# Strassen's scheme for every token pair of the last down projection

## The chip, the core and the metric

The kernel runs on one core of a Trainium2 chip. The core has a matrix engine (TensorE, "PE" in the profile), a vector engine (VectorE, "DVE"), a scalar engine (ScalarE, "ACT"), GpSimd ("POOL") and SyncE ("SP"), which here issues the transfers. Each engine takes its instructions in their order and waits on semaphores that other engines or transfers raise. The metric is the device time of one execution in microseconds (us); the time of a kernel is the median over its runs.

## The reference

One transformer block over 2048 tokens of width 1024, all inputs in bfloat16:

```python
mod = (_silu(c) @ w_mod).reshape(c.shape[0], 6, 1, -1)      # sa, ca, ga, sb, cb, gb
h = _layernorm(x) * (1 + ca) + sa
x = x + ga * _A_ref(h, A_wqkv, A_wo)      # linear attention, 32 heads of 32
h = _layernorm(x) * (1 + cb) + sb
x = x + gb * _B_ref(h, B_w_gate, B_w_up, B_w_down)
# _B_ref: _gelu(x @ w_gate) * (x @ w_up) @ w_down
```

The feed-forward network (FFN) has an inner width of 3584: `w_gate` and `w_up` are 1024 x 3584, `w_down` is 3584 x 1024. The change concerns the last product, the multiplication by `w_down` (the down projection), for the second half of the tokens.

## The kernel before

All engines' work is recorded by a small scheduler class (`Sched`): every operation names the bytes that it reads and writes, and the semaphore waits follow from that. Within an engine the order of the recorded calls is the order of execution (one early stretch of the program is reordered by a planner; the part that matters here is not). On-chip memory is one arena with offsets given by hand (`OFF_...`), so many tiles share bytes over time: a tile can be written when the last reader of what lay there is done.

The 2048 tokens are 16 chunks of 128 (c0 to c15). After attention, the FFN runs in two halves `p` of 1024 tokens. A half first runs 14 units `u`, each for 256 of the 3584 inner columns, and then the down projection of its eight chunks, with `w_down` cut into 28 K tiles of 128 rows (`fc`), loaded as seven tiles `wd0` to `wd6` of four K tiles, 1 MB each (`wd_dma`).

**A unit** (`unit`, L1449 on) multiplies by Strassen's scheme in Winograd's form: operands are cut 2 x 2, seven products take the place of eight, and sums of blocks are formed before and after. TensorE runs the products in the order 1, 5, 6, 2, 7, 3, 4, each for gate and up (t = 0, 1) with four matmuls of 512 columns (L1426). Products 1 and 2 use blocks as they are, in bf16; the others use sums, kept in fp32r. VectorE makes the weight sums of the next unit (`t_sum`, L1401), the additions after products 6 and 7 (`padd`, L1437) and the products yT = gelu(gate) * up (L1446); ScalarE makes the gelu (L1442), copies of partial results (L1431, L1434) and the fp32r copy of one weight block (L1390). The result `yT` stays on chip as the stationary operand of the down projection.

**The loads of w_down in the second half.** `wd0` and `wd1` are still on chip from the first half. `wd2` lies on the buffer of the gate and up weights of the last unit but one and is loaded behind that unit. `wd5`, `wd3`, `wd6` and `wd4` are issued in this order at the end of the last unit. Each waits until the tile below it has been read: `wd5` until product 6, `wd3` until product 2, `wd6` until product 3, `wd4` until product 4.

**The down projection of the second half** (the `if p:` branch) works on pairs of chunks; a pair has four results of 128 x 512 (two chunks by two halves of the output), each in one PSUM bank, so two pairs fill the eight banks. The first pair (c8, c9) is direct: for `wd0`, `wd1`, `wd2`, `wd5`, `wd3`, `wd6`, `wd4` in turn, 16 matmuls each (`down`, L1511). Meanwhile VectorE forms the weight sums `dt` (`d_t`, L1540) of K tiles 0 to 11 and, for the next pair, the sums of `yT` (`d_s`, L1567). The other three pairs (`d_pair`) run those 12 K tiles by Strassen's scheme: the K tiles are taken in six pairs (`NDJ = 6`), rows and columns being the two chunks, the two K tiles of a pair and the two halves of the output; seven products (`d_prod`, L1581) of six matmuls each make 42 in place of 48. The other 16 K tiles are added directly, 64 matmuls. After product 1 ScalarE copies the result to a second bank (L1599), after product 5 it copies to the tile `de` (L1601), and VectorE adds after products 6 and 7 (`d_add`, L1589). A finished bank is multiplied by the gate, added to x (`evac`, L1503 and L1504), and stored (L1506). In the last pair the last bank is cut into pieces of 320, 128 and 64 columns (`TAIL`), so that little remains behind the last matmul.

The tiles of the sums: `dt` has 15 tiles of 2 x 512 fp32r, `ds0` and `ds1` hold the first two sums of `yT`, and the other three of `yT` lie in `dha` and `dhb`, the right halves of `wd0`, `wd1` and `wd2`, whose direct reading is over by then.

Of the kernel before, what the change touches and what calls it, by code (L numbers as in the profile page):

```python
# [319 lines left out]
def bass_adaLN_cond__linear_attn_block__geglu_ffn__prompt_kernel(  # L320
# [16 lines left out]
    with ExitStack() as es:  # L337
# [1170 lines left out]
        def down(c_, k, b, c0, c1, fcs, first, last):  # L1508
            ci, n, o = c_ % (2 * CPG), c1 - c0, None
            for fc in fcs:  # L1510
                o = sch.op(T, lambda e, fc=fc: e.matmul(PS(b, 0, n), YT[:, yrow(fc), ci * P:(ci + 1) * P], WDT[fc // 4][:, fc % 4, c0:c1],  # L1511
                                                        start=first and fc == fcs[0], stop=last and fc == fcs[-1], skip_group_check=True),
                           rd=r_yt(fc, ci * P, (ci + 1) * P) + r_wd(fc), pwr=(pr(b) if first and fc == fcs[0] else ()), note=f"down c{c_} k{k} fc{fc}")
# [13 lines left out]
        def r_dt(q, i):  # L1527
            return [(OFF_DT[q][i], OFF_DT[q][i] + 4096, f"dt{q}{i}")]

        def d_t(q, i):  # L1530
            w = WDT[q].ap().rearrange("p (j r) d -> p j r d", r=2)
            b = lambda r, cc: w[:, :, r, cc * 512:(cc + 1) * 512]
            rb_ = lambda r, cc: [(WDQ[q] + (2 * j + r) * 2048 + cc * 1024, WDQ[q] + (2 * j + r) * 2048 + (cc + 1) * 1024, f"wd{q}") for j in range(2)]
            t32 = lambda k: DT[q][k].ap().bitcast(f32)
# [5 lines left out]
            sch.op(V, lambda e: e.tensor_tensor(DT[q][i][:], in0, in1, ALU.subtract), rd=rd, wr=r_dt(q, i), note=f"dtsum {q}.{i}")  # L1540
# [244 lines left out]
```

## Time and profile before

| | |
|---|---|
| median of 3 runs | 798.46 us (798.2 to 798.8) |
| profiled execution | 798.54 us |
| its span, first to last instruction | 796.3 us |
| TensorE busy | 789.3 us (99%), 3987 matmuls |
| VectorE busy | 595.8 us (75%) |
| ScalarE busy | 312.2 us (39%) |
| FFN units of the second half | up to 699.2 us, 12.6 each |
| down projection of the second half | 699.2 to the end |

How the lines are read: "L1511 PE MATMUL ps_all<-wd,yT ..." names the line of the kernel, the engine, the operation, the tile written and the tiles read. A group's line gives the count, the busy time, the mean of one in ns, and the idle time of the engine ahead of it with what ended it. In the timeline a row is: start, duration, engine, line, operation, shape, count, and in brackets the idle time before it. The chain of work that ended last is followed back from the last instruction: at each step to what released it, or to the instruction ahead of it on its engine; in order of time a row is start, duration, engine and line. Matmuls are pipelined, so a matmul's duration (379 ns) is longer than the time from one start to the next; times of a stream are therefore taken from the chain or from starts.

### The profile page before, as it was taken

Reading aid. Unit: us, or ns where it says so; the run is one execution under the profiler, and the core shown is the slowest. Engines: PE = TensorE matmul, PEld = TensorE weight load, DVE = VectorE, ACT = ScalarE, POOL = GpSimd, SP = SyncE. Lnnn points to the kernel's source line nnn. Section 1 sums busy time; section 2 is a strip of 40 time slices with the busy share of each in tenths; the row PEclk is TensorE's granted clock in tenths of the full one; section 3 lists DMA queues with packets and bytes.
Section 4 is the critical chain, followed back from the end, with each engine's and each line's share of the span. In section 5 each row is a group of like instructions: output and inputs, shape, how many; then the busy total and the mean of one; then the engine's idle time right before and its main releaser. Section 6 shows DMA issues by size and latency. Waiting matters only on the chain.

```text
span 796.3 us, 10865 instructions
## 1 busy us (share of the span) xinstructions
PE 789.3 (99%) x3987; PEld 470.2 (59%) x3987; DVE 595.8 (75%) x1046; ACT 312.2 (39%) x526; POOL 40.4 (5%) x102
## 2 busy tenths in 40 slices
PE   8999999999999999999999999999999999999998
PEld 4444445666445776767775444467776777745555
DVE  6799898894889978878776374577878878885433
ACT  2497743333574434444353411033534444321000
POOL 2121200000420000000001000000000000000000
PEclk9999999999999999999999999999999999999999
DMA  9789849849996153323228234022332323340000
GB/s 287 242 177 234 172 110 243 196 89 203 221 266 183 54 152 112 106 55 104 83 77 244 47 80 106 20 87 74 86 103 56 107 55 104 106 158 28 27 27 26
DMA packets 161340, 97.72 MB, mean 123 GB/s; under 512 B 68476, under 2 KB 148612, under 8 KB 160264
## 3 DMA queue, kind: packets, MB, share of 16 engines
q1 hardware_dynamic: 161272, 97.04, 47.4%
q8 instruction: 31, 0.51, 0.3%
q14 instruction: 21, 0.17, 0.1%
q10 hardware_dynamic: 16, 0.00, 0.0%
HBM read 78.92 MB, written 4.47 MB: 105 GB/s over the span
## 4 chain that ended last, share of the span: by engine, by line
PE 94%; DVE 2%; SPq 2%; DMA 1%; issue 0%; DVEq 0%
PE ps_all L1426 44%; PE ps_all L1511 20%; PE ps_all L883 7%; PE ps_all L919 7%; PE ps_all L868 6%; PE ps_all L1252 5%; PE ps_all L1581 4%; SPq L585 1%; DMA wmq<-in_w_mod_dram 1%; DVE xall L1266 1%; SPq L590 1%; DVE tp L1401 0%; PE ps_all L901 0%; PE ps_all L1184 0%; DVE ss L1381 0%
## 5 line engine op out<-in xcount | busy, mean ns | idle before, releaser
L1426 PE MATMUL ps_all<-ss,tp 128*128 128x512 f32 x896 | 224.4, 402 | 0.4 <-DVE ss L1381 0.4
L1426 PEld LDWEIGHTS ps_all<-ss,tp 128*128 128x128 f32 x896 | 168.3, 188 | 41.0 <-DVE ss L1381 1.1
L1511 PE MATMUL ps_all<-wd,yT 128*128 128x512 bf16 (+3 forms) x784 | 163.3, 370 | 0.0
L1511 PEld LDWEIGHTS ps_all<-wd,yT 128*128 128x128 bf16 x784 | 74.7, 98 | 87.8 <-issue 0.8
L1442 ACT ACTIVATE ge<-ps_all 128x512 f32<-128x512 f32 x112 | 64.1, 597 | 142.8 <-DVE ps_all L1437 81.0
L1426 PE MATMUL ps_all<-h2a,wt 128*128 128x512 bf16 x448 | 106.3, 380 | 0.0
L1401 DVE TENSOR_TENSOR tp<-wt 128x512 fp32r<-128x512 bf16 x112 | 74.5, 687 | 42.0 <-PE ps_all L1426 20.8
L1446 DVE TENSOR_TENSOR yT<-ge,ps_all 128x512 bf16<-128x512 f32 x112 | 74.4, 684 | 32.8 <-PE ps_all L1426 29.4
L1437 DVE TENSOR_TENSOR ps_all<-ps_all,es 128x512 f32<-128x512 f32 x112 | 75.0, 694 | 13.3 <-PE ps_all L1426 13.2
L1401 DVE TENSOR_TENSOR tp<-wt,tp 128x512 fp32r<-128x512 bf16 x112 | 71.9, 683 | 0.0
L1426 PEld LDWEIGHTS ps_all<-h2a,wt 128*128 128x128 bf16 x448 | 39.4, 98 | 54.3 <-issue 13.8
L868 PE MATMUL ps_all<-wk,h1T 128*128 128x512 bf16 x248 | 56.9, 379 | 0.4 <-DVE h1T L711 0.2
L919 PE MATMUL ps_all<-h1T,wq 128*128 128x512 bf16 x256 | 56.7, 379 | 0.0
L1252 PE MATMUL ps_all<-w,pq 128*128 128x512 bf16 x256 | 56.3, 379 | 0.0
L1426 PE MATMUL ps_all<-ar,tp 128*128 128x512 f32 x224 | 55.3, 389 | 0.0
L1503 DVE TENSOR_TENSOR ps_all<-ps_all,gbb 128x512 f32<-128x512 f32 (+3 forms) x34 | 22.6, 664 | 43.0 <-PE ps_all L1511 43.0
L1431 ACT ACTIVATE ps_all<-ps_all 128x512 f32<-128x512 f32 x56 | 32.6, 582 | 54.6 <-PE ps_all L1426 52.6
L857 ACT ACTIVATE eb<-ps_all 128x512 f32<-128x512 f32 x64 | 36.3, 593 | 36.9 <-PE ps_all L868 14.2
L1426 PEld LDWEIGHTS ps_all<-ar,tp 128*128 128x128 f32 x224 | 42.0, 188 | 8.8
L919 PEld LDWEIGHTS ps_all<-h1T,wq 128*128 128x128 bf16 x256 | 25.0, 98 | 30.0
L1252 PEld LDWEIGHTS ps_all<-w,pq 128*128 128x128 bf16 x256 | 24.7, 98 | 30.0 <-ACT w L1186 0.3
L1434 ACT ACTIVATE es<-ps_all 128x512 f32<-128x512 f32 x56 | 33.5, 601 | 18.3 <-PE ps_all L1426 17.3
(140 smaller groups left out, 733.4 us busy)
## 6 DMA issues: line engine op xcount, KB each, us to landing
wt<-in_B_w_gate_dram SPq DMA_DIRECT2D x28, 512.0 KB, 4.1
wt<-in_B_w_up_dram SPq DMA_DIRECT2D x28, 512.0 KB, 5.1
wd<-in_B_w_down_dram SPq DMA_DIRECT2D x12, 1024.0 KB, 7.4
rb<-scr_rd SPq DMA_DIRECT2D x32, 256.0 KB, 6.6
...
```

Of the source, the lines that this page charges most:

```text
L857: sch.op(A, lambda e: e.activation(EB[i][:, :], PS(bank), ACTF.Exp), prd=pr(bank), wr=rng, note=f"{note}.exp")
L868: o = sch.op(T, lambda e, dc=dc: e.matmul(PS(bank), H1[sg][:, ci, dc, :], W_[:, dc, jg * 512:(jg + 1) * 512], start=(dc == 0), stop=(dc == ...
L883: o = sch.op(T, lambda e, c_=c_: e.matmul(PS(bank, 0, n), PK[c_][:, g * P:(g + 1) * P], xrow(c_, o_, o_ + n), start=(c_ == 0), stop=(c_ == ...
L919: o = sch.op(T, lambda e, dc=dc: e.matmul(PS(b), WQ[:, dc, qc * P:(qc + 1) * P], H1[sg][:, :, dc, :], start=(dc == 0), stop=(dc == NDC - 1 ...
L1252: last[half] = sch.op(T, lambda e, g=g, half=half: e.matmul(PS(b0 + half), PQ[sg][:, g, ci * P:(ci + 1) * P], W2[:, g, half * 512:(half + ...
L1401: sch.op(V, lambda e, t=t: e.tensor_tensor(TP[k][:, t, :, :], in0[:, t, :, :], in1[:, t, :, :], ALU.subtract), rd=r0[t:t + 1] + (r1[t:t + ...
L1426: o = sch.op(T, lambda e, l_=l_, r_=r_, dc=dc: e.matmul(PS(b), l_, r_, start=fresh and dc == 0, stop=dc == ND2 - 1, skip_group_check=True) ...
L1434: sch.op(A, lambda e: e.activation(ES[t][:, :], PS(BE + t), ACTF.Copy), prd=pr(BE + t), wr=r_2k(OFF_ES[t], f"es{t}"), note="escp")
L1437: sch.op(V, lambda e: e.tensor_tensor(PS(dst + t), PS(BB + t), ES[t][:, :], ALU.add), prd=pr(BB + t), rd=r_2k(OFF_ES[t], f"es{t}"), pwr=pr ...
L1442: sch.op(A, lambda e: e.activation(GE[i][:, :], PS(b), ACTF.Gelu_apprx_tanh), prd=pr(b), wr=r_2k(OFF_GE[i], f"ge{i}"), note="gelu")
L1446: sch.op(V, lambda e: e.tensor_tensor(YT[:, yrow(fc), h * SGW:(h + 1) * SGW], GE[i][:, :], PS(b + 1), ALU.mult), rd=r_2k(OFF_GE[i], f"ge{i ...
L1511: o = sch.op(T, lambda e, fc=fc: e.matmul(PS(b, 0, n), YT[:, yrow(fc), ci * P:(ci + 1) * P], WDT[fc // 4][:, fc % 4, c0:c1], start=first a ...
```

## The change

All four pairs of the second half go through `d_pair`, and the scheme takes 14 K tiles in seven pairs (`NDJ = 7`): all of `wd0`, `wd1`, `wd2` and the first half of `wd3`. A pair then has 49 Strassen matmuls and 56 direct ones (K tiles 14 to 27).

- The first pair starts with direct matmuls: of `wd5` (16), `wd3` (8) and `wd6` (16), into banks 0 to 3. ScalarE copies these partial results (`d_part`) into two tiles `dm` that lie on rows of `yT` no longer needed, and VectorE adds them (`d_merge`) to the Strassen results in banks 4 to 7 after products 2, 7, 3 and 4. Then come the 16 matmuls of `wd4`, with banks in the order 0, 3, 1, 2. Its evictions are put off (`later`) into the next pair.
- The first two kinds of weight sums (i = 0, 1) of `wd0` and `wd1` are formed as eight sums of one row each in units 5 to 12 of the second half; the last unit forms two of `wd2` and one of `wd0`. The rest is formed after the last unit. `dt` has four tiles for each `wd` tile in use (i = 0 to 3).
- The fourth weight sum (i = 4, product 4) is written into the right half of `wd0` to `wd3` itself (`dh`), as two runs of 256 fp32r values in a row, after the other readers of that half.
- The sums of `yT` have three tiles `ds` for five sums; sums 3 and 4 are formed inside their own pair, after products 5 and 6, and each sum is split into six K-tile pairs and one.
- In the other pairs the direct part follows the block, as it did; in the last one the tail pieces go into banks 3, 4 and 5.

The diff, cut to its core:

```diff
-NDJ = 6
-OFF_DT = [[OFF_XALL, OFF_XALL + 4096, OFF_R3, OFF_R3 + 4096, OFF_R3 + 8192],
-          [OFF_R3 + 12288, OFF_HT + 24576, OFF_HT + 28672, OFF_R3 + 16384, OFF_R3 + 20480],
-          [OFF_GUH, OFF_GUH + 4096, OFF_R3 + 24576, OFF_ROW, OFF_GAB]]
-OFF_DS = [OFF_XALL + 8192, OFF_XALL + 8192 + NDJ * 512]
-OFF_DE = OFF_XALL + 8192 + NDJ * 1024
+NDJ = 7
+OFF_DT = [[OFF_XALL, OFF_XALL + 4096, OFF_R3 + 8192, OFF_GUH],
+          [OFF_XALL + 8192, OFF_XALL + 12288, OFF_R3 + 16384, OFF_GUH + 4096],
+          [OFF_R3, OFF_R3 + 4096, OFF_R3 + 20480, OFF_R3 + 24576],
+          [OFF_ROW, OFF_ROW + 2048, OFF_GAB, OFF_GAB + 2048]]
+OFF_DS = [OFF_HT + 24576, OFF_HT + 28672, OFF_R3 + 12288]
+OFF_DE = OFF_SMALL
...
-        DT = [[at(f"dt{q}{i}", [P, 2, 512], f32r, OFF_DT[q][i]) for i in range(5)] for q in range(3)]
-        DS = [at(f"ds{i}", [P, NDJ, P], f32r, OFF_DS[i]) for i in range(2)]
+        NJQ = [2, 2, 2, 1]
+        DT = [[at(f"dt{q}{i}", [P, NJQ[q], 512], f32r, OFF_DT[q][i]) for i in range(4)] for q in range(4)]
+        DH = [at(f"dh{q}", [P, NJQ[q], 2, 512], f32r, WDQ[q]) for q in range(4)]
+        DS = [at(f"ds{i}", [P, NDJ, P], f32r, OFF_DS[i]) for i in range(3)]
         DE = at("de", [P, 512], f32, OFF_DE)
-        DH = [at("dha", [P, 4, 2, 512], f32r, HBO[1]), at("dhb", [P, 2, 2, 512], f32r, OFF_WS)]
...
+            if i == 4:
+                return DH[q][:, j0:j1, :, 256:512], r_wh(q, 0, 1, f"dh{q}", j0, j1) + r_wh(q, 1, 1, f"dh{q}", j0, j1)
+            return DT[q][i][:, j0:j1, :], [(OFF_DT[q][i] + j0 * 2048, OFF_DT[q][i] + j1 * 2048, f"dt{q}{i}")]
...
+        def d_t(i, q, j0=0, j1=2):
+            j1 = min(j1, NJQ[q])
+            w = WDT[q][:, 2 * j0:2 * j1, :].rearrange("p (j r) d -> p j r d", r=2)
+            b = lambda r, cc: (w[:, :, r, cc * 512:(cc + 1) * 512], r_wh(q, r, cc, f"wd{q}", j0, j1))
+            t32 = lambda k: (dt_ap(q, k, j0, j1)[0].bitcast(f32), dt_ap(q, k, j0, j1)[1])
+            dst, wr = dt_ap(q, i, j0, j1)
             if i == 3:
-                sch.op(A, lambda e: e.activation(DT[q][3][:], b(1, 1), ACTF.Copy), rd=rb_(1, 1), wr=r_dt(q, 3), note=f"dtcp {q}")
+                src, rd = b(1, 1)
+                sch.op(A, lambda e: e.activation(dst, src, ACTF.Copy), rd=rd, wr=wr, note=f"dtcp {q}")
                 return
-            in0, in1, rd = ((b(0, 1), b(0, 0), rb_(0, 1) + rb_(0, 0)), (b(1, 1), t32(0), rb_(1, 1) + r_dt(q, 0)),
-                            (b(1, 1), b(0, 1), rb_(1, 1) + rb_(0, 1)), None, (b(1, 0), t32(1), rb_(1, 0) + r_dt(q, 1)))[i]
-            sch.op(V, lambda e: e.tensor_tensor(DT[q][i][:], in0, in1, ALU.subtract), rd=rd, wr=r_dt(q, i), note=f"dtsum {q}.{i}")
-
-        DHS = {2: (0, 0), 3: (0, 1), 4: (1, 0)}
+            (in0, r0), (in1, r1) = ((b(0, 1), b(0, 0)), (b(1, 1), t32(0)), (b(1, 1), b(0, 1)), None, (b(1, 0), t32(1)))[i]
+            if i == 4:
+                in0, in1 = (t_.rearrange("p j (h c) -> p j h c", h=2) for t_ in (in0, in1))
+            sch.op(V, lambda e: e.tensor_tensor(dst, in0, in1, ALU.subtract), rd=r0 + r1, wr=wr, note=f"{'dtsum' if j1 - j0 == 2 else 'dtone'} {q}.{i}")
...
+        DSB = (0, 1, 2, 0, 1)
...
-            if i < 2:
-                return DS[i][:, j0:j1, :], [(OFF_DS[i] + j0 * 512, OFF_DS[i] + j1 * 512, f"ds{i}")]
-            r, sl = DHS[i]
-            h, o_, base = (0, 0, HBO[1]) if j1 <= 4 else (1, 4, OFF_WS)
-            return (DH[h][:, j0 - o_:j1 - o_, r, 256 + sl * P:256 + (sl + 1) * P],
-                    [(base + (2 * (j - o_) + r) * 2048 + 1024 + sl * 512, base + (2 * (j - o_) + r) * 2048 + 1536 + sl * 512, f"dh{i}") for j in range(j0, j1)])
+            k = DSB[i]
+            return DS[k][:, j0:j1, :], [(OFF_DS[k] + j0 * 512, OFF_DS[k] + j1 * 512, f"ds{k}")]
...
-        def d_s(ca, cb, i):
-            for j0, j1 in (((0, NDJ),) if i < 2 else ((0, 4), (4, NDJ))):
+        def d_s(ca, i):
+            cb = ca + 1
+            for j0, j1 in ((0, 6), (6, NDJ)):
                 dst, wr = ds_ap(i, j0, j1)
                 if i == 4:
...
+            i = {1: None, 2: None, 5: 0, 6: 1, 7: 2, 3: 3, 4: 4}[k]
+            dst = PS(b).rearrange("p (h c) -> p h c", h=2) if i == 4 else PS(b)
...
-                if k in (1, 2):
+                q, jj = divmod(j, 2)
+                if i is None:
                     l_, rl = y_ap(ca, k - 1, j, j + 1)
-                    fc = 2 * j + k - 1
-                    r_, rr = WDT[fc // 4][:, fc % 4, 0:512], [(WDQ[fc // 4] + fc % 4 * 2048, WDQ[fc // 4] + fc % 4 * 2048 + 1024, f"wd{fc // 4}")]
+                    r_, rr = WDT[q][:, 2 * jj + k - 1, 0:512], [(WDQ[q] + (2 * jj + k - 1) * 2048, WDQ[q] + (2 * jj + k - 1) * 2048 + 1024, f"wd{q}")]
                 else:
-                    l_, rl = ds_ap({5: 0, 6: 1, 7: 2, 3: 3, 4: 4}[k], j, j + 1)
-                    ti = {5: 0, 6: 1, 7: 2, 3: 3, 4: 4}[k]
-                    r_, rr = DT[j // 2][ti][:, j % 2, :], [(OFF_DT[j // 2][ti] + j % 2 * 2048, OFF_DT[j // 2][ti] + j % 2 * 2048 + 2048, f"dt{j // 2}{ti}")]
-                o = sch.op(T, lambda e, l_=l_, r_=r_, j=j: e.matmul(PS(b), l_[:, 0, :], r_, start=k in (1, 5) and j == 0, stop=j == NDJ - 1, skip_group_check=True),
+                    l_, rl = ds_ap(i, j, j + 1)
+                    t_, rr = dt_ap(q, i)
+                    r_ = t_[:, jj]
+                o = sch.op(T, lambda e, l_=l_, r_=r_, j=j: e.matmul(dst, l_[:, 0, :], r_, start=k in (1, 5) and j == 0, stop=j == NDJ - 1, skip_group_check=True),
...
-        TAIL = ((7, 0, 320), (0, 320, 448), (1, 448, 512))
-
-        def d_pair(ca, nxt):
-            b0 = 2 * (ca % CPG)
+        DM = [at(f"dm{i}", [P, 4, SP2 // 2], f32, OFF_YT + (8 + 4 * i) * SP2 * 2) for i in range(2)]
+
+        def dm(i):
+            o_ = OFF_YT + (8 + 4 * i) * SP2 * 2
+            return DM[i][:, :, 0:P], [(o_ + r * SP2 * 2, o_ + r * SP2 * 2 + 512, f"dm{i}") for r in range(4)]
+
+        def sq4(ap):
+            return ap.rearrange("p (a b) -> p a b", a=4)
+
+        def d_part(i, a):
+            dst, wr = dm(i)
+            sch.op(A, lambda e: e.activation(dst, sq4(PS(a)), ACTF.Copy), prd=pr(a), wr=wr, note="dmcp")
+
+        def d_merge(i, b):
+            src, rd = dm(i)
+            sch.op(V, lambda e: e.tensor_tensor(sq4(PS(b)), sq4(PS(b)), src, ALU.add), prd=pr(b), rd=rd, pwr=pr(b), note="dmerge")
+
+        TAIL = ((3, 0, 320), (4, 320, 448), (5, 448, 512))
+
+        later = []
+
+        def d_pair(ca):
+            i0 = (ca - 2 * CPG) // 2
+            b0 = 0 if i0 % 2 else 4
+            pre, last = i0 == 0, i0 == 3
+            fcs = list(range(2 * NDJ, NFC))
+            fcs = [fc for q in (5, 3, 6, 4) for fc in fcs if fc // 4 == q]
+            if pre:
+                for q in (5, 3, 6):
+                    for n in range(4):
+                        down(ca + n // 2, n % 2, n, n % 2 * 512, n % 2 * 512 + 512, [fc for fc in fcs if fc // 4 == q], q == 5, q == 6)
+                for i, n in enumerate((0, 3)):
+                    d_part(i, n)
             for k in (1, 5, 6, 2, 7, 3, 4):
                 d_prod(ca, b0, k)
+                if k in (1, 6, 7):
+                    mine = later[:2 if k == 1 else 1]
+                    del later[:2 if k == 1 else 1]
                 if k == 1:
+                    for x in mine:
+                        evac(*x)
                     sch.op(A, lambda e: e.activation(PS(b0 + 2), PS(b0), ACTF.Copy), prd=pr(b0), pwr=pr(b0 + 2), note="dpcp")
                 elif k == 5:
                     sch.op(A, lambda e: e.activation(DE[:, :], PS(b0 + 3), ACTF.Copy), prd=pr(b0 + 3), wr=R_DE, note="descp")
+                    d_s(ca, 3)
                 elif k == 6:
+                    d_s(ca, 4)
                     d_add(b0, ((b0 + 1, 0, 512),))
+                    if pre:
+                        d_t(4, 2)
+                        d_t(4, 3)
                 elif k == 7:
-                    d_add(b0, ((b0 + 3, 0, 512),) if nxt else TAIL)
-            if nxt:
-                for i in range(5):
-                    d_s(ca + 2, ca + 3, i)
-                for q in (3, 5, 6, 4):
-                    for c_ in (ca, ca + 1):
-                        down_q(c_, (q,), last=q == 4)
+                    d_add(b0, TAIL if last else ((b0 + 3, 0, 512),))
+                if k in (6, 7):
+                    for x in mine:
+                        evac(*x)
+                if pre and k in (2, 7, 3, 4):
+                    i, n = {2: (0, 0), 7: (1, 3), 3: (0, 1), 4: (1, 2)}[k]
+                    d_merge(i, b0 + n)
+                    if k in (2, 7):
+                        d_part(i, {2: 1, 7: 2}[k])
+            if not last:
+                for i in (0, 2, 1) if pre else range(3):
+                    d_s(ca + 2, i)
+                for q in (4,) if pre else (3, 5, 6, 4):
+                    for n in (0, 3, 1, 2) if pre else range(4):
+                        down(ca + n // 2, n % 2, b0 + n, n % 2 * 512, n % 2 * 512 + 512, [fc for fc in fcs if fc // 4 == q], False, q == 4, q == (4 if pre else 3))
+                for n in (0, 3, 1, 2) if pre else range(4):
+                    x = (ca + n // 2, n % 2, b0 + n, n % 2 * 512, n % 2 * 512 + 512)
+                    if pre:
+                        later.append(x)
+                    else:
+                        evac(*x)
                 return
-            fcs = list(range(2 * NDJ, NFC))
-            for k in range(2):
-                down(ca, k, b0 + k, k * 512, (k + 1) * 512, fcs, False, True)
-                evac(ca, k, b0 + k, k * 512, (k + 1) * 512)
-            for k, (b, k0, k1) in enumerate(((b0 + 2, 0, 512),) + tuple((b, c0 + 512, c1 + 512) for b, c0, c1 in TAIL)):
-                down(ca + 1, k, b, k0, k1, fcs, False, True)
-                evac(ca + 1, k, b, k0, k1)
+            for n, (b, k0, k1) in enumerate(((b0, 0, 512), (b0 + 1, 512, 1024), (b0 + 2, 0, 512)) + tuple((b, c0 + 512, c1 + 512) for b, c0, c1 in TAIL)):
+                c_, k = (ca, n) if n < 2 else (ca + 1, n - 2)
+                down(c_, k, b, k0, k1, fcs, False, True, True)
+                evac(c_, k, b, k0, k1)
...
-        ORD1 = (1, lambda: d_t(0, 0), 5, lambda: d_t(0, 1), 6, 2, lambda: d_t(0, 2), 7, 3, lambda: (d_t(0, 3), d_t(0, 4)), 4)
+        ORD1 = {NFP - 1: (1, 5, lambda: d_t(0, 2), 6, 2, lambda: d_t(1, 2), 7, 3, lambda: d_t(2, 0), 4)}
+        for n in range(8):
+            ORD1[NFP - 9 + n] = (1, lambda n=n: d_t(n // 2 % 2, n // 4, n % 2, n % 2 + 1), 5, 6, 2, 7, 3, 4)
...
-                unit(p, u, *([ORD0] if p == u == 0 else [ORD1] if p and u == NFP - 1 else []))
+                unit(p, u, *([ORD0] if p == u == 0 else [ORD1[u]] if p and u in ORD1 else []))
...
-                for q, i in [(1, i) for i in range(5)] + [(2, i) for i in range(5)]:
-                    d_t(q, i)
-                for q in (0, 1, 2):
-                    for c_ in (c0, c0 + 1):
-                        down_q(c_, (q,), first=q == 0)
-                for i in range(5):
-                    d_s(c0 + 2, c0 + 3, i)
-                for q in (5, 3, 6, 4):
-                    for c_ in (c0, c0 + 1):
-                        down_q(c_, (q,), last=q == 4)
-                for c_ in (c0 + 2, c0 + 4, c0 + 6):
-                    d_pair(c_, c_ + 2 < NCH)
+                d_s(c0, 0)
+                d_t(2, 1)
+                d_s(c0, 1)
+                d_t(2, 2)
+                d_s(c0, 2)
+                for q in range(4):
+                    d_t(3, q)
+                for i in range(3):
+                    d_t(i, 3)
+                d_t(4, 0)
+                d_t(4, 1)
+                for c_ in range(c0, c0 + 2 * CPG, 2):
+                    d_pair(c_)
```

More of the change, by code (lines that the diff above doesn't have):

```diff
@@ L1506, in evac, with down @@
             sch.dma(Q, lambda e: e.dma_start(out_v[:, c_, c0:c1], XALL[:, c_, c0:c1]), rd=r_x(c_, c0, c1), note=f"out{c_}.{k}")
-        def down(c_, k, b, c0, c1, fcs, first, last):
+        def down(c_, k, b, c0, c1, fcs, first, last, after=False):
             ci, n, o = c_ % (2 * CPG), c1 - c0, None
@@ L1512, in down @@
                                                         start=first and fc == fcs[0], stop=last and fc == fcs[-1], skip_group_check=True),
-                           rd=r_yt(fc, ci * P, (ci + 1) * P) + r_wd(fc), pwr=(pr(b) if first and fc == fcs[0] else ()), note=f"down c{c_} k{k} fc{fc}")
+                           rd=r_yt(fc, ci * P, (ci + 1) * P) + r_wd(fc), pwr=(pr(b) if (first or after) and fc == fcs[0] else ()), note=f"down c{c_} k{k} fc{fc}", overwrite_ok=after)
             if last:
@@ L1526, in bass_adaLN_cond__linear_attn_block__geglu_ffn__prompt_kernel, with r_wh @@
         pq_scale(2, 0, GH[0] + GH[1])
[L1527 to L1534, printed above, removed]
+        def r_wh(q, r, cc, name, j0=0, j1=2):
+            return [(WDQ[q] + (2 * j + r) * 2048 + cc * 1024, WDQ[q] + (2 * j + r) * 2048 + (cc + 1) * 1024, name) for j in range(j0, min(j1, NJQ[q]))]
@@ new lines, in dt_ap @@
+        def dt_ap(q, i, j0=0, j1=2):
+            j1 = min(j1, NJQ[q])
[3 more added lines that the diff above has]
+        def d_t(i, q, j0=0, j1=2):
+            j1 = min(j1, NJQ[q])
+            w = WDT[q][:, 2 * j0:2 * j1, :].rearrange("p (j r) d -> p j r d", r=2)
+            b = lambda r, cc: (w[:, :, r, cc * 512:(cc + 1) * 512], r_wh(q, r, cc, f"wd{q}", j0, j1))
+            t32 = lambda k: (dt_ap(q, k, j0, j1)[0].bitcast(f32), dt_ap(q, k, j0, j1)[1])
+            dst, wr = dt_ap(q, i, j0, j1)
@@ L1566, in d_s @@
                                             (y_ap(ca, 0, j0, j1), y_ap(cb, 0, j0, j1), ALU.subtract), (y_ap(ca, 1, j0, j1), s_(1), ALU.subtract))[i]
-                sch.op(V, lambda e, dst=dst, in0=in0, in1=in1, op=op: e.tensor_tensor(dst, in0, in1, op), rd=r0 + r1, wr=wr, note=f"dssum{i} {cb}")
+                sch.op(V, lambda e, dst=dst, in0=in0, in1=in1, op=op: e.tensor_tensor(dst, in0, in1, op), rd=r0 + r1, wr=wr, note=f"{'dssum' if j0 == 0 else 'dsone'}{i} {cb}")
         def d_prod(ca, b0, k):
             b = b0 + {1: 0, 2: 0, 5: 3, 6: 2, 7: 2, 4: 2, 3: 1}[k]
+            i = {1: None, 2: None, 5: 0, 6: 1, 7: 2, 3: 3, 4: 4}[k]
+            dst = PS(b).rearrange("p (h c) -> p h c", h=2) if i == 4 else PS(b)
             o = None
             for j in range(NDJ):
-                if k in (1, 2):
+                q, jj = divmod(j, 2)
+                if i is None:
                     l_, rl = y_ap(ca, k - 1, j, j + 1)
-                    fc = 2 * j + k - 1
-                    r_, rr = WDT[fc // 4][:, fc % 4, 0:512], [(WDQ[fc // 4] + fc % 4 * 2048, WDQ[fc // 4] + fc % 4 * 2048 + 1024, f"wd{fc // 4}")]
-                else:
-                    l_, rl = ds_ap({5: 0, 6: 1, 7: 2, 3: 3, 4: 4}[k], j, j + 1)
-                    ti = {5: 0, 6: 1, 7: 2, 3: 3, 4: 4}[k]
-                    r_, rr = DT[j // 2][ti][:, j % 2, :], [(OFF_DT[j // 2][ti] + j % 2 * 2048, OFF_DT[j // 2][ti] + j % 2 * 2048 + 2048, f"dt{j // 2}{ti}")]
-                o = sch.op(T, lambda e, l_=l_, r_=r_, j=j: e.matmul(PS(b), l_[:, 0, :], r_, start=k in (1, 5) and j == 0, stop=j == NDJ - 1, skip_group_check=True),
+                    r_, rr = WDT[q][:, 2 * jj + k - 1, 0:512], [(WDQ[q] + (2 * jj + k - 1) * 2048, WDQ[q] + (2 * jj + k - 1) * 2048 + 1024, f"wd{q}")]
+                else:
+                    l_, rl = ds_ap(i, j, j + 1)
+                    t_, rr = dt_ap(q, i)
+                    r_ = t_[:, jj]
+                o = sch.op(T, lambda e, l_=l_, r_=r_, j=j: e.matmul(dst, l_[:, 0, :], r_, start=k in (1, 5) and j == 0, stop=j == NDJ - 1, skip_group_check=True),
                            rd=rl + rr, pwr=(pr(b) if j == 0 else ()), note=f"down P{k} c{ca} j{j}", overwrite_ok=True)
```

## The prediction

> **What bounds the kernel now.** I read the page's busy shares first, then the chain of work that ended last, then that chain in order of time for the last 120 us (before that the change adds only sums on the vector engine, from 585 us on), and only then the vector engine's and the queue's timelines at the places where something is put in or pulled forward.
>
> ```profile
> PE 789.3 (99%) x3987; PEld 470.2 (59%) x3987; DVE 595.8 (75%) x1046; ACT 312.2 (39%) x526; POOL 40.4 (5%) x102
> ...
> PE 94%; DVE 2%; SPq 2%; DMA 1%; issue 0%; DVEq 0%
> ```
>
> TensorE is busy nearly all the time and carries 94% of the chain. So a change of matrix products is worth what it takes out of TensorE's own stream, less any wait that it puts in. The chain between 680 us and the end:
>
> ```profile
> 679.80 19.57 PE ps_all L1426 x87
> 699.38 24.19 PE ps_all L1511 x112
> 723.57 9.50 PE ps_all L1581 x42
> 733.07 13.83 PE ps_all L1511 x64
> 746.90 9.50 PE ps_all L1581 x42
> 756.41 13.83 PE ps_all L1511 x64
> 770.24 9.50 PE ps_all L1581 x42
> 779.74 12.56 PE ps_all L1511 x64
> 792.30 0.02 issue
> 792.33 0.51 DVE ps_all L1503
> ```
>
> The reader sees the four pairs of token chunks: the first direct (112 matmuls of L1511), three with 42 Strassen matmuls (L1581) and 64 direct ones. Nothing but TensorE stands in it until 792.30, where the end's evictions follow the 320-wide piece. The granted clock in this stretch is 1.00. I work against the profiled execution, 798.54 us (span 796.3 and 2.2 around it); the median, 798.46, is 0.08 below it.
>
> **1. The matmuls.** Direct: 24.19 / 112 = 0.216 us each. A Strassen block of 42 has 12 bf16 matmuls (products 1 and 2) and 30 fp32r: 9.50 - 12 x 0.216 = 6.91, or 0.230 for an fp32r matmul, its share of the changes of type included. With seven K-tile pairs a block is 14 bf16 and 35 fp32r: 9.50 + 2 x 0.216 + 5 x 0.230 = 11.08. The direct rest falls from 16 to 14 K tiles, 56 x 0.216 = 12.10. A pair is then 23.18 us.
> - First pair (c8, c9): 24.19 to 23.18, -1.01.
> - Second and third: 9.50 + 13.83 = 23.33 to 23.18, -0.15 each.
> - Last pair, up to the end of the 320-wide piece: 9.50 + 12.56 = 22.06. Of the direct part 6 wide matmuls go and 2 of 320 columns, at (12.56 - 48 x 0.216) / 16 = 0.137: -1.57. The block is 1.58 longer. +0.01. The 128- and 64-wide pieces run beside the evictions of the one before, as now.
>
> Sum -1.30. If all the difference between the types sat in the changes of type, of which a block has as many as before, the five new fp32r matmuls would cost 0.216 and the sum would be -1.30 - 4 x 5 x 0.014 = -1.6; that is the low end. The gain is small because 35 of 49 matmuls are dearer than the 56 they replace: eight direct ones (1.73 us) become seven (1.58).
>
> The Trainium skill, "TensorE: Matmul & The Clock Gate", section "Back-to-back issue gap", gives a warm gap by the number of columns alone, about 216 ns for 512, whatever the type. The direct rows agree (0.216), the Strassen rows don't (0.230). By the page the four blocks would save about 2 us as an estimate, by the rows 1.3; the rows decide.
>
> **2. Weight sums in the FFN units.** Units 5 to 12 of the second half each get one 512-wide sum (`d_t` with one of two rows) behind the fourth weight sum. One unit of the vector engine now:
>
> ```profile
> 675.03 1.28 DVE L1401 TENSOR_TENSOR tp<-wt,tp 128x512 fp32r<-128x512 bf16 x2
> 676.95 0.69 DVE L1401 TENSOR_TENSOR tp<-wt 128x512 fp32r<-128x512 bf16 x1 [0.64 <-PE ps_all L1426]
> 677.87 0.69 DVE L1401 TENSOR_TENSOR tp<-wt 128x512 fp32r<-128x512 bf16 x1 [0.23 <-PE ps_all L1426]
> 678.77 0.70 DVE L1437 TENSOR_TENSOR ps_all<-ps_all,es 128x512 f32<-128x512 f32 x1 [0.21 <-PE ps_all L1426]
> ```
>
> The new sum takes 0.69 (0.60 from start to start) and goes into the idle 0.64 between the first two rows; what is queued behind it are the next unit's first sums, with 0.23 and 0.21 idle behind them again. Zero. Without that gap it would be 8 x 0.6 = 5 us at most, but only if TensorE waited for each, and nothing in the chain's units shows it waiting for the vector engine. The last unit has no sums for a next unit; it gets three 1024-wide sums (1.13 from start to start) where four stood. Zero.
>
> **3. The direct matmuls at the front of the down projection.** This is the one wait that I expect. Now the first pair begins with `wd0`, `wd1`, `wd2` and reaches `wd6` 80 matmuls (17.3 us) after the last unit. In the changed kernel it begins with `wd5` (16 matmuls) and two tiles of `wd3` (8), and the 25th needs `wd6`. The loads themselves, their order on the queue and what they wait for stay.
>
> ```profile
> 699.22 24.35 PE L1511 MATMUL ps_all<-wd,yT 128*128 128x512 bf16 x112
> ```
> ```profile
> L1335 SPq DMA_DIRECT2D wd<-in_B_w_down_dram x1: 367/367/367, 697.6 to 697.6; - x1
> ...
> DMA to landing us min/median/max: 7.4/7.4/7.4
> ```
>
> The load of `wd6` is issued at 697.60, when product 3 of the last unit has read the tile under it, and lands 7.4 later, at 705.0. TensorE would want it at 699.22 + 24 x 0.216 = 704.40: a wait of 0.6. `wd5` (issued 692.26, 5.2 to landing) is there 1.8 early, `wd3` (issued at 693.99; its landing is not recorded; at the longest time of the five, 8.2, at 702.2) before 702.68. Ends: nothing, if `wd6` takes the loads' median of 6.3; 1.4, if it takes 8.2. I take the row itself, +0.6.
>
> The Trainium skill, "DMA: Bandwidth & Descriptors", section "Queues, rings and completion order", says that on each DMA engine the descriptors of a queue are consumed in ring order. The 7.4 beside the 5.2 of `wd5` agrees: `wd6` stands behind `wd3`. A load alone at `wd5`'s 5.2 would land at 702.8 with no wait, and the whole sum would be -1.3 instead of -0.7.
>
> **4. The vector engine at the front of the first pair.** It has had 24.2 us of direct matmuls ahead of the first Strassen block; now it has 40 matmuls, 8.64 us.
>
> ```profile
> 698.36 1.22 DVE L1540 TENSOR_TENSOR dt<-wd,dt 128x1024 fp32r<-128x1024 bf16 x1
> 699.49 0.68 DVE L1446 TENSOR_TENSOR yT<-ge,ps_all 128x512 bf16<-128x512 f32 x1
> ...
> 710.40 0.96 DVE L1567 TENSOR_TENSOR ds<-ds,yT 128x768 fp32r<-128x768 f32 x1
> 711.28 0.68 DVE L1567 TENSOR_TENSOR dha<-yT 128x512 fp32r<-128x512 bf16 x1
> ```
>
> Start to start: 1.13 for 1024, 0.88 for 768, 0.60 for 512; the new 128-wide piece 0.3, from the 0.29 of the last evictions. After the last y product (free at 700.09) come `ds0`, a 1024 sum, `ds1`, a 1024 sum, `ds2` (each `ds` 1.2), done at 705.95; three sums of `wd3` at 706.55, 707.15, 707.75; two fourth sums, 710.0. TensorE starts product 1 at 699.22 + 8.64 + 0.6 = 708.46, product 5 at 709.97 (needs the sum of 706.55: 3.4 to spare), product 6 at 711.58 (4.4), product 7 at 714.70. Then `ds` sum 3 waits for product 5's reads and is done at 712.6; queued behind it is the addition after product 6, ready from 713.6 and done at 714.3, 0.4 ahead of product 7. The last two fourth sums end at 716.0, product 4 starts at 717.92: 1.9. The merge of the last bank ends at 720.7, `wd4` matmuls reach that bank at 722.1. Zero, with 1.9 as the least margin of new work. The 0.4 is 0.2 more than the margin now, since product 2 between is a matmul longer. ScalarE's partial copies, 0.6 each, stand beside the same 8.64 and beside products 2 to 4.
>
> **5. Product 4 reads its moving operand in two runs of 256 fp32r values** (the fourth sums lie in unread halves of `w_down`). No row shows this for fp32r. The nearest:
>
> ```profile
> L868 PE MATMUL ps_all<-wk,h1T 128*128 128x512 bf16 x248 | 56.9, 379 | 0.4 <-DVE h1T L711 0.2
> L919 PE MATMUL ps_all<-h1T,wq 128*128 128x512 bf16 x256 | 56.7, 379 | 0.0
> ```
>
> L868 streams a row of `wk` in one run, L919 streams `h1T` in four runs of 128: 379 both. I take zero. Upper end: another step as from bf16 to fp32r, 28 x 0.014 = 0.4; a gain is excluded, since the same 512 columns stream.
>
> **6. Later pairs.** The first pair's evictions (8 x 0.7) move into the second pair, behind its first sums and additions; later ones stay behind the direct matmuls. Each pair's vector work (four `ds` 4.8, two additions 1.4, evictions 5.5) is 11.7 of 23.2. The output stores move by some 4 us on the queue; only the end waits for them. Zero.
>
> **Sum.** -1.30 + 0.6 = -0.7: span 795.6, 797.84 on the profiled execution's scale, 797.8 against the median.
>
> **The rivals.**
> - *`wd6` is there in time.* For it: 6.3 is the median of these loads, and 0.6 is small. Against: its own row. Then -1.3: 797.2. With the low end of step 1, 796.8.
> - *`wd6` later.* At the 8.2 of the load behind it, 1.4: 798.6. With step 5's upper end 799.0.
> - *Slower: two runs cost product 4 its rate.* Place: 28 matmuls, seven in each pair, all on the chain. Against it stand the two rows of step 5; for it, that they are bf16. At double time, 28 x 0.23 = 6.4: 804.2. It decides from 0.08 us a matmul on (28 x 0.08 = 2.3 above my forecast).
> - *Slower: the vector engine is late at the front.* Were all sums of step 4 half as long again, the two fourth sums would end at 715.0, `ds` sum 3 at 716.8 and the addition at 717.5, and product 7, due at 714.7, would wait 2.8: 800.6, just across; from 1.4 times on it decides. Against it: the same forms ran in 1.22, 0.96 and 0.68 under the same four loads now.
> - *The change does not do what it says:* excluded on TensorE, whose stream falls from 3987 to 3973 matmuls.
>
> **How the numbers follow.** No change can be told within 0.2%, 1.6 us here: 796.9 to 800.1. Chances: my forecast (a wait of 0.3 to 1.0) 0.48, 797.4 to 798.3; no wait 0.22, 0.08 of it below 796.9 by the low end of step 1; a longer wait 0.14; product 4 at a lower rate 0.07; the vector engine late 0.05; something unseen 0.04. Slower takes the 0.07, the 0.04 and the 0.05, whose large cases are unknown: 0.16. Faster 0.08, same 0.76. The range, 796.9 to 799.4, reaches over the longer wait and the bounds of steps 3 and 5.
>
> **What would show it.** In the chain: first pair about 23.2 plus the wait, blocks of 49 in 11.1, direct runs of 56 in 12.1. TensorE idle about 0.6 at 704 to 705, the only idle time before the end, released by the load of `wd`. The vector engine's units with no idle 0.64. Product 4's matmuls at the mean of products 3 and 7. The prediction is wrong if the first products of the first pair wait for the vector engine, if product 4 stands out, or if a 49-block takes 10.8 or 11.5.

## The result and the profile after

| | before | changed |
|---|---|---|
| median | 798.47 us (797.57 to 799.89, 22 runs) | 797.12 us (796.52 to 798.53, 22 runs) |
| profiled execution, span | 796.3 us | 794.5 us |

The ratio is 0.9985, with a 95% interval of 0.9979 to 0.9992: by it 1.2 us less, between 0.6 and 1.7 (the medians differ by 1.35). The forecast was 797.8, with a range of 796.9 to 799.4. The median lies in the range, but outside the 797.4 to 798.3 that the forecast gave for its own case, a wait of 0.3 to 1.0, and close to the 797.2 of the rival without a wait.

The page of the changed kernel, busy shares and the chain:

```profile
PE 783.7 (99%) x3908; PEld 473.6 (60%) x3973; DVE 609.2 (77%) x1074; ACT 317.6 (40%) x535; POOL 40.2 (5%) x102
...
PE 90%; SPq 4%; DVE 3%; DMA 1%; issue 1%; POOL 0%; ACT 0%; POOLq 0%; DVEq 0%
```

There are 3973 weight loads, as many as matmuls in the program, but 3908 records of matmuls: 65 are missing from this trace. The pieces "issue 0.07" below are such gaps, not waits. The chain in order of time, down projection of the second half:

```profile
698.99 3.90 PE ps_all L1513 x18
...
707.64 11.04 PE ps_all L1591 x49
...
722.15 11.04 PE ps_all L1591 x49
...
745.29 11.04 PE ps_all L1591 x49
...
768.43 11.04 PE ps_all L1591 x49
...
779.53 10.93 PE ps_all L1513 x55
790.46 0.02 issue
790.49 0.51 DVE ps_all L1505
```

Four blocks of 49 stand where three of 42 stood, each 11.04, and the end begins at 790.49 in place of 792.33. The starts of the pairs, in the timeline of before and then of after (before, the first pair starts at 699.22):

```profile
723.41 1.46 PE L1581 MATMUL ps_all<-wd,yT 128*128 128x512 bf16 x6
746.74 1.46 PE L1581 MATMUL ps_all<-wd,yT 128*128 128x512 bf16 x6
770.07 1.46 PE L1581 MATMUL ps_all<-wd,yT 128*128 128x512 bf16 x6
```
```profile
698.84 8.81 PE L1513 MATMUL ps_all<-wd,yT 128*128 128x512 bf16 x39
721.99 1.67 PE L1591 MATMUL ps_all<-wd,yT 128*128 128x512 bf16 x7
745.12 1.67 PE L1591 MATMUL ps_all<-wd,yT 128*128 128x512 bf16 x7
768.26 1.67 PE L1591 MATMUL ps_all<-wd,yT 128*128 128x512 bf16 x7
```

By these the pairs of the changed kernel take 23.15, 23.13, 23.14 and, to the first tail eviction, 22.23. Before they took 24.19, 23.33, 23.33 and 22.26. Pair by pair: -1.04, -0.20, -0.19, -0.03, in all -1.46. The other 0.4 of the span's 1.8 lies ahead of the changed stretch (698.84 against 699.22 for the same matmul), where the changed kernel does the same TensorE work; in the traces below that part varies by 1.4.

So in this trace the forecast wait of 0.6 is missing. The load of `wd6`, on the line that issues it:

```profile
L1337 SPq DMA_DIRECT2D wd<-in_B_w_down_dram x1: 368/368/368, 697.2 to 697.2; - x1
...
DMA to landing us min/median/max: 5.4/5.4/5.4
```

It landed after 5.4 us, not 7.4. The 25th matmul wants it 1.6 + 24 x 0.216 = 6.8 after its issue. Whether this is the rule or luck was the first question.

### The profile page after: what moved, and what is told of

It is laid out like the page before. It is cut to its first block, busy times and chain, and to the rows that moved or that the text cites. A ratio compares the mean times of both kernels' runs of the same rounds, so it can differ in the third digit from the quotient of the medians.

```text
span 794.5 us, 10828 instructions
## 1 busy us (share of the span) xinstructions
PE 783.7 (99%) x3908; PEld 473.6 (60%) x3973; DVE 609.2 (77%) x1074; ACT 317.6 (40%) x535; POOL 40.2 (5%) x102
## 4 chain that ended last, share of the span: by engine, by line
PE 90%; SPq 4%; DVE 3%; DMA 1%; issue 1%; POOL 0%; ACT 0%; POOLq 0%; DVEq 0%
PE ps_all L1428 44%; PE ps_all L1513 18%; PE ps_all L885 7%; PE ps_all L921 7%; PE ps_all L1591 6%; PE ps_all L870 6%; PE ps_all L1254 2%; SPq L587 1%; DVE xall L1268 1%; SPq L592 1%; SPq L692 1%; DMA wt<-in_B_w_up_dram 1%; DMA wk<-in_A_wqkv_dram 1%; DVE tp L1403 0%; PE ps_all L1186 0%
## 5 line engine op out<-in xcount | busy, mean ns | idle before, releaser
L1513 PE MATMUL ps_all<-wd,yT 128*128 128x512 bf16 (+3 forms) x684 | 144.6, 370 | 0.9
L1513 PEld LDWEIGHTS ps_all<-wd,yT 128*128 128x128 bf16 x700 | 66.6, 98 | 78.6 <-issue 1.3
L1428 PE MATMUL ps_all<-h2a,wt 128*128 128x512 bf16 x420 | 100.1, 380 | 1.9
L870 PE MATMUL ps_all<-wk,h1T 128*128 128x512 bf16 x239 | 55.3, 379 | 1.2 <-DMA wk<-in_A_wqkv_dram 0.7
L870 PEld LDWEIGHTS ps_all<-wk,h1T 128*128 128x128 bf16 x248 | 23.5, 98 | 29.0 <-DVE h1T L713 2.5
```

The costliest lines, as they stand in the source:

```text
L870: o = sch.op(T, lambda e, dc=dc: e.matmul(PS(bank), H1[sg][:, ci, dc, :], W_[:, dc, jg * 512:(jg + 1) * 512], start=(dc == 0), stop=(dc == ...
L1428: o = sch.op(T, lambda e, l_=l_, r_=r_, dc=dc: e.matmul(PS(b), l_, r_, start=fresh and dc == 0, stop=dc == ND2 - 1, skip_group_check=True) ...
```

## The experiments

Whole times have intervals of about 0.7 us either way, too wide for single terms. Traces are compared by a *stretch*: from the start of the last unit's last matmul (0.23 ahead of the first direct one) to the first tail eviction (320 wide). It is 93.33 before and 91.88 in the first trace of the changed kernel. The reading that the experiments test: the matmuls save 1.4, and the wait for `wd6` is its landing less 6.8 where that is positive. In the expectations of experiments 1, 2 and 4, theory A is that the load is in time, as in the first trace of the changed kernel; theory B is that it is late, as in the trace of before, and that the first trace was a lucky one.

### 1. The changed kernel again (no edit)

> The changed kernel once more, for a second trace of the load of wd6. Theory A (the load is in time): wd6 lands 5 to 6 us after its issue, TensorE has no idle time before its first wd6 matmul, time 1.2 to 1.5 below the kernel before. Theory B (the load is late as in the trace of before, 7.4 us, and the first trace was a lucky one): idle 0.3 to 1.0 there, time 0.6 to 0.9 below.

Measured: 797.26 us against 798.47, ratio 0.9983 (0.9974 to 0.9992). TensorE's timeline and the load in this trace:

```profile
699.10 5.35 PE L1513 MATMUL ps_all<-wd,yT 128*128 128x512 bf16 x24
704.99 3.63 PE L1513 MATMUL ps_all<-wd,yT 128*128 128x512 bf16 x16 [0.54 <-DMA wd<-in_B_w_down_dram]
```
```profile
697.48 7.47 DMA wd<-in_B_w_down_dram
704.95 0.05 issue
704.99 3.63 PE ps_all L1513 x16
```

The second fence is the chain: the transfer stands in it for 7.47 us. TensorE stops behind the 24th matmul, as forecast. From start to start the 25th is 0.92 behind the 24th, 0.70 more than a matmul's 0.216 (the bracket's 0.54 counts from the 24th's modelled end). The stretch is 92.61, 0.73 more than in the first trace. So for this execution theory B holds in the trace, the wait as forecast. In the time it does not: 1.2 below the kernel before is what theory A expected (1.2 to 1.5), not B (0.6 to 0.9), and the median is 797.26 here against 797.12 in the first comparison.

### 2. All four pairs, over 12 K tiles

```diff
-NDJ = 7
+NDJ = 6
-            for j0, j1 in ((0, 6), (6, NDJ)):
+            for j0, j1 in ((0, NDJ),):
-                        d_t(4, 3)
-                for q in range(4):
+                for q in range(3):
                     d_t(3, q)
-                for i in range(3):
-                    d_t(i, 3)
```

> All four pairs by the scheme, but over 12 K tiles as before (42 + 64 matmuls a pair). By the sum of the prediction: first pair 24.19 to 23.33, the others unchanged, so 0.86 below the kernel before; the first wd6 matmul stands 32 behind the start (6.9 us), so no wait for the load under either theory. If the gain came from the longer blocks alone, no difference from the kernel before.

Measured: 798.10 us, ratio 0.9995 (0.9986 to 1.0004); the stretch is 92.70, 0.63 below before. No wait for `wd6`. The 0.2 short of 0.86 is one place:

```profile
709.36 9.50 PE ps_all L1591 x42
...
722.33 9.71 PE ps_all L1591 x42
```

The second block's product 7 waited 0.2 for the addition after product 6. That addition starts 0.50 behind the start of product 6's last matmul in the other pairs and 0.86 here; why, is open. With six matmuls in product 2, there is next to no room for such a delay. So moving the first pair to the scheme is the larger part of the gain.

### 3. Three pairs, over 14 K tiles

The first pair is direct, in the order `wd0` to `wd3`, `wd5`, `wd6`, `wd4`:

```diff
+                for q in (0, 1, 2, 3, 5, 6, 4):
+                    for n in range(4):
+                        down(c0 + n // 2, n % 2, 4 + n, n % 2 * 512, n % 2 * 512 + 512, range(4 * q, 4 * q + 4), q == 0, q == 4)
...
-                for c_ in range(c0, c0 + 2 * CPG, 2):
+                for c_ in range(c0 + 2, c0 + 2 * CPG, 2):
                     d_pair(c_)
```

> The first pair direct over all 28 K tiles as before, the other three pairs by the scheme over 14 K tiles. By the prediction's fp32r matmul of 0.230: 0.15 saved in each of two pairs, nothing in the last, 0.3 below the kernel before. By the 0.227 that matmuls far into a run of fp32r show in the trace after: 0.2 each, 0.4 below. If moving the first pair is what brings all of it: no difference.

Measured: 798.29 us, ratio 0.9995 (0.9987 to 1.0004); the stretch is 93.05, 0.28 below before, 0.11 of it lost again at one gap between two direct matmuls near 701, whose cause the trace does not name. Without that gap 0.39, as with 0.227 for an added fp32r matmul. Experiments 2 and 3 together, with their two small losses taken out, give 0.84 and 0.39; the first pair's own longer block, 0.18, makes up 1.4.

### 4. `wd6` wanted 1.73 earlier

```diff
-                for q in (5, 3, 6):
+                for q in (5, 6, 3):
                     for n in range(4):
-                        down(ca + n // 2, n % 2, n, n % 2 * 512, n % 2 * 512 + 512, [fc for fc in fcs if fc // 4 == q], q == 5, q == 6)
+                        down(ca + n // 2, n % 2, n, n % 2 * 512, n % 2 * 512 + 512, [fc for fc in fcs if fc // 4 == q], q == 5, q == 3)
```

> The front of the first pair in the order wd5, wd6, wd3: wd6 is wanted 8 matmuls (1.73 us) earlier. Theory A, landing as in the trace after (5.4 us from issue, 3.8 us behind the first wd5 matmul, which wants it 3.46 behind): idle 0.3 to 0.5, time 0.4 above the changed kernel. Theory B, 7.4 us from issue: idle 2.3, time about 1.7 above the changed kernel.

```profile
699.42 3.63 PE L1513 MATMUL ps_all<-wd,yT 128*128 128x512 bf16 x16
705.39 5.35 PE L1513 MATMUL ps_all<-wd,yT 128*128 128x512 bf16 x24 [2.34 <-DMA wd<-in_B_w_down_dram]
```

The load landed 7.55 after its issue; TensorE lost 2.51 from start to start, the stretch is 94.41, 2.53 above the first trace of the changed kernel. 798.75 us, ratio 1.0002 (0.9993 to 1.0011), 1.5 above experiment 1 on the same chip. So the lateness of this load is paid in full here. The landings of this load up to here are 7.40 (before), 5.40, 7.47 and 7.55, and 6.58 and 6.57 in experiments 2 and 3, where nothing waits for it: 5.4 is the lowest of them.

### 5. The changed kernel a third time (no edit)

> The changed kernel a third time, beside the next three. If the wait for wd6 comes and goes with the landing of the load (5.4 us from issue in one trace, 7.5 in the other; it is wanted 6.8 after the issue), TensorE idles there by landing less 6.8 where that is positive, and the stretch from the last unit's last matmul to the first tail eviction is 91.9 plus that. If the first trace was an exception: 0.6 to 0.8 of idle time again.

Measured: 797.47 us against 798.68, ratio 0.9986 (0.9977 to 0.9995). Landing 7.62, idle 0.85, stretch 92.72 = 91.88 + 0.84.

### 6. The load of `wd6` in two halves

```diff
+        def wd_half(q, h):
+            f0 = q * 4 + 2 * h
+            sch.dma(Q, lambda e: e.dma_start(WDT[q][:, 2 * h:2 * h + 2, :], wd_v[:, f0:f0 + 2, :]),
+                    wr=r_wd(f0) + r_wd(f0 + 1), note=f"wd{q}")
...
-                wd_dma(q)
+                if p and q == 6:
+                    wd_half(6, 0)
+                    wd_half(6, 1)
+                else:
+                    wd_dma(q)
...
-                for q in (5, 3, 6):
+                for g in ((20, 21, 22, 23), (14, 15), (24, 25), (26, 27)):
                     for n in range(4):
-                        down(ca + n // 2, n % 2, n, n % 2 * 512, n % 2 * 512 + 512, [fc for fc in fcs if fc // 4 == q], q == 5, q == 6)
+                        down(ca + n // 2, n % 2, n, n % 2 * 512, n % 2 * 512 + 512, g, g[0] == 20, g[0] == 26)
```

> The load of wd6 in two halves, the first issued when product 7 (not 3) of the last unit is done, and the first pair's front in the order wd5, wd3, first half of wd6, second half. If the wait is what remains of the prediction's step 3, it goes: the second half is wanted 1.73 us later than wd6 was, so idle time only beyond 8.5 us from issue; the stretch is 91.9 whatever the landing, and the time is 0.2 to 0.5 below the changed kernel. If the halves land later for sharing the queue with the loads around them: idle 0.3 or more at one of the two, and no gain.

Measured: 796.94 us (796.56 to 797.41) against 798.68, ratio 0.9976 (0.9966 to 0.9985). In the chain of this kernel nothing but TensorE and the gaps of missing records:

```profile
699.57 3.90 PE ps_all L1518 x18
703.47 0.05 issue
703.52 4.70 PE ps_all L1518 x21
708.22 11.04 PE ps_all L1596 x49
```

The two halves (each with its landing) and the direct matmuls of the first pair, without idle time among them:

```profile
L1342 SPq DMA_DIRECT2D wd<-in_B_w_down_dram x1: 367/367/367, 696.0 to 696.0; - x1
DMA to landing us min/median/max: 8.0/8.0/8.0
...
L1342 SPq DMA_DIRECT2D wd<-in_B_w_down_dram x1: 368/368/368, 697.8 to 697.8; - x1
DMA to landing us min/median/max: 7.5/7.5/7.5
...
699.41 8.81 PE L1518 MATMUL ps_all<-wd,yT 128*128 128x512 bf16 x39
```

The halves landed 8.00 and 7.54 after their issues (at 695.97 and 697.78), no sooner than the whole did in experiments 1, 4 and 5 (7.47 to 7.62). The edit does two things. The first half waits only until product 7 of the last unit, and not until product 3, so it is issued 1.8 earlier than the whole was, against the first direct matmul; it is wanted at the same place and is there 0.6 ahead. The second half is issued where the whole was and is wanted 8 matmuls later, 1.0 behind its landing. At the place where the whole was wanted the second half would have been 0.7 late, and the first half, with its 8.0 from the later issue, 1.2. The stretch is 91.88, that of the changed kernel's trace without a wait.

### 7. Three more sums at the front of the first pair

```diff
                 d_s(c0, 0)
-                d_t(2, 1)
+                for _ in range(4):
+                    d_t(2, 1)
```

> Three more 1024-wide weight sums at the front of the first pair (3.4 us of vector work). By the margins of the prediction's step 4, less the wait that it reckoned with: product 5 waits 0.5, the addition after product 6 comes 1.2 late, so TensorE loses 1.2 in all where wd6 is in time and less where it is late. If the vector engine were the bound at the front: 3.4 lost.

```profile
709.43 3.56 PE L1591 MATMUL ps_all<-dt,ds 128*128 128x512 f32 x14
712.83 1.69 PE L1591 MATMUL ps_all<-wd,yT 128*128 128x512 bf16 x7
715.60 3.49 PE L1591 MATMUL ps_all<-dt,ds 128*128 128x512 f32 x14 [1.09 <-DVE ps_all L1599]
```

The load landed 5.40 after its issue here, no wait for it. TensorE lost 1.25 ahead of product 7, behind the addition (L1599), and 0.12 more behind the next matmul; the stretch is 93.25, 1.37 above 91.88. 798.62 us, ratio 0.9997 (0.9989 to 1.0006). The 1.2 is right in sum and the place only half: product 5 did not wait. The sum of `wd3` is the seventh K-tile pair and is wanted only by a product's last matmul, 1.4 later than I had it.

### 8. Each unit's sum three times

```diff
-            ORD1[NFP - 9 + n] = (1, lambda n=n: d_t(n // 2 % 2, n // 4, n % 2, n % 2 + 1), 5, 6, 2, 7, 3, 4)
+            ORD1[NFP - 9 + n] = (1, lambda n=n: [d_t(n // 2 % 2, n // 4, n % 2, n % 2 + 1) for _ in range(3)], 5, 6, 2, 7, 3, 4)
```

> Each of the eight sums in the units made three times (1.2 us more of vector work in each of eight units). If the cover is only the idle 0.64 that the prediction named, each unit is 0.6 to 1.2 longer: 5 to 10 us above the changed kernel. If the unit's whole idle time counts (0.64 + 0.23 + 0.21 + 0.19 + 1.06 = 2.3, of which the change uses 0.6): no difference.

```profile
675.92 2.13 DVE L1551 TENSOR_TENSOR dt<-wd,dt 128x512 fp32r<-128x512 bf16 x3
677.97 1.29 DVE L1403 TENSOR_TENSOR tp<-wt 128x512 fp32r<-128x512 bf16 x2
679.18 1.29 DVE L1439 TENSOR_TENSOR ps_all<-ps_all,es 128x512 f32<-128x512 f32 x2
681.11 0.69 DVE L1448 TENSOR_TENSOR yT<-ge,ps_all 128x512 bf16<-128x512 f32 x1 [0.64 <-PE ps_all L1428]
```

Measured: 797.29 us, ratio 0.9981 (0.9972 to 0.9990), no different from the changed kernel. Of the four idle pieces that the changed kernel has in a unit (0.23, 0.21, 0.19 and 1.06) three are gone, 0.64 of the fourth is left, and TensorE does not wait in the units. The stretch, with a landing of 7.46 and an idle 0.69, is 92.60.

### 9 and 10. The split load and the changed kernel once more, side by side (no further edit)

> The split load of wd6 once more, for the interval. No idle time before the wd6 matmuls, time about 1.5 below the kernel before and 0.3 to 0.5 below the changed kernel. If the earlier difference to the changed kernel was chance: none now.

> The changed kernel beside it. The wait for wd6 0 or 0.6 to 0.9 by the landing of the load; time 1.1 to 1.4 below the kernel before.

Measured against 798.71: the split load 797.18 us (796.36 to 797.82), ratio 0.9979 (0.9970 to 0.9988); the changed kernel 797.61 us (796.69 to 798.95), ratio 0.9984 (0.9975 to 0.9992). Stretches 91.88 without idle time and 92.36 with 0.46 (landing 7.23). The difference, 0.4, is close to the one of experiments 5 and 6 (0.5). The intervals against the kernel before overlap, but they are not the comparison that counts: run against run on the same chip, the split load's mean is 0.85 (experiments 5 and 6) and 0.48 (9 and 10) below the changed kernel's, 0.7 together with a 95% interval of 0.4 to 1.0 (runs drawn again at random). Both traces of the split load are without a wait and three of the changed kernel's four have one. The load in the chains of experiments 10, 8, 5 and 4:

```profile
697.64 7.23 DMA wd<-in_B_w_down_dram
...
697.28 7.46 DMA wd<-in_B_w_down_dram
...
697.30 7.62 DMA wd<-in_B_w_down_dram
...
697.79 7.55 DMA wd<-in_B_w_down_dram
```

### The wait, trace by trace

| trace | landing of `wd6` after issue | idle before its first matmul | stretch |
|---|---|---|---|
| changed kernel, first | 5.40 | 0 | 91.88 |
| experiment 10 | 7.23 | 0.46 | 92.36 |
| experiment 8 (sums tripled) | 7.46 | 0.69 | 92.60 |
| experiment 1 | 7.47 | 0.70 | 92.61 |
| experiment 5 | 7.62 | 0.85 | 92.72 |
| experiment 4 (wanted 1.73 earlier) | 7.55 | 2.51 | 94.41 |

Experiment 7 had a landing of 5.40 and no wait for it. In the first five rows the idle time is the landing less 6.8 to within 0.04, and the stretch is 91.88 and the idle time to within 0.03.

## Why the prediction was right, and where it was off

- **Step 1, the matmuls.** Forecast -1.30, measured -1.45 (stretch without a wait). The pairs' terms -1.01, -0.15, -0.15, +0.01 came out at -1.04, -0.20, -0.19, -0.03. The mis-sized term is the five added fp32r matmuls: not 0.230 but (11.04 - 9.50 - 2 x 0.216) / 5 = 0.222, which brings 0.04 in each block. The traces give two parts of it. From start to start the fp32r matmuls of a run take 0.224 to 0.236 at first (behind its first step) and 0.227 later, and an added one stands late in its run: 0.227, about a third of the difference. The rest goes with the front of the runs: nearly all runs of the changed kernel settle at 0.227 after six or seven matmuls, where those of the kernel before took about ten; why is open. The Trainium skill ("TensorE: Matmul & The Clock Gate", section "Back-to-back issue gap") gives the warm gap of an isolated matmul by columns alone, about 216 ns for 512: that agrees with the direct rows here (0.216) and not with the fp32r ones. By it the gain would have been 2.0, as an estimate.
- **Step 2, the units' sums.** Zero, right. The cover is larger than the gap that the step named: experiment 8 put in three times the work and TensorE lost nothing.
- **Step 3, the wait for `wd6`.** Forecast +0.6, from one row. In the four traces of the changed kernel itself, 0, 0.46, 0.70 and 0.85: 0.5 in the mean. The wait and its place stand: experiment 4 pays the earlier need in full, and experiments 6 and 9 remove the wait and the stretch's excess. The size was one draw of a load that varies: in the ten traces that load `wd6` whole it landed 5.4 to 7.6 after its issue, four times before the 6.8 at which the changed kernel wants it and six times after. So the rival "there in time" is right for some executions, the first trace among them. The reason that the step gave for the 7.4, the place behind `wd3` in the queue, is not enough: at the same place the load also landed at 5.40, close to `wd5`'s 5.2.
- **Step 4, the front.** Zero, right. The margin that counts is the addition after product 6, which the step had at 0.4 behind a wait of 1.0 for product 6. In the trace after:

```profile
710.58 1.16 DVE L1575 TENSOR_TENSOR ds<-yT,ds 128x768 fp32r<-128x768 bf16 x2 [1.11 <-PE ps_all L1591]
712.47 0.70 DVE L1599 TENSOR_TENSOR ps_all<-ps_all,de 128x512 f32<-128x512 f32 x1 [0.72 <-PE ps_all L1591]
```

  VectorE is idle for 1.11 and 0.72 up to that addition, which ends 0.37 before product 7 starts: 2.2 in all. Experiment 7 agrees: 3.4 us of sums cost 1.4, so about 2 are free. The step was wrong to let product 5 need the sums of `wd3` at its start.
- **Step 5, two runs of 256.** Zero, right, and so the rival on the other side falls. Products by form in the trace after:

```profile
L1591 PE MATMUL ps_all<-dh,ds x28: 388/389/389, 716.9 to 779.1; 128*128 128x512 f32 x28
```

  All 28 matmuls of product 4 lie at 388 to 389 ns, the median of those with a contiguous operand (389), and seven of them span 1.75 us in the timeline, (1.75 - 0.39) / 6 = 0.227 from start to start.
- **Step 6, later pairs.** Zero, right: the third and fourth pair lose nothing.

The sum by what was measured is -1.45 + 0.5 = -0.95, against -0.7 forecast. The medians of the four comparisons are 1.35, 1.21, 1.21 and 1.10 lower; their intervals hold 0.95. All four lie nearer to the -1.3 of the rival without a wait than to the forecast, and yet three of the four traces have the wait. Both errors point the same way: step 1 saved 0.15 more than forecast, and the wait is there in a part of the executions only. So the number was 0.4 to 0.65 too high, and it is the range that held.

What remains, 0.15 to 0.4, is open. Part of it can be that the load lands in time more often when nothing is profiled. Unprofiled runs have no record of the load, but experiment 4, which pays all of its lateness, gives an estimate: by its ratio it is 0.2 above the kernel before, where without a wait it would be 1.45 below, so the wait is about 1.65 and the landing 5.1 + 1.65 = 6.7 after the issue, give or take 0.7, against 7.55 in its trace. Part of it can be chance or something outside the stretch: the split load, without a wait, is 1.74 and 1.53 below the kernel before by the medians, where its stretch gives 1.45, and its intervals hold 1.45 too. The spread of the times decides nothing: the kernel before, which does not wait for `wd6`, spreads from 797.6 to 800.1.

The profile also holds the sixteen steps by which the semaphore of a load rises. In the ten traces that load `wd6` whole the first step comes 4.9 to 5.2 after the issue. The last comes 0.3 and 0.4 behind the first in the two traces with 5.40, and 1.4 to 2.5 behind it in the other eight; in experiment 1 fifteen steps have come by 5.33 and the sixteenth comes at 7.47. So the load starts to land at about the same time in all of them, and it is its last steps that are late. The Trainium skill, "DMA: Bandwidth & Descriptors", section "Why a DMA increments its semaphore by 16 and not by 1", says that a transfer runs on up to 16 engines that finish independently and counts as landed only when all have finished; the steps agree with that. What holds the last ones back in some executions is open.
